# Reordering a scheduled MLP kernel: tile 1 ahead of tiles 2 and 3 at the start, and block 1's layer norm and w2's block sums in other places

## The chip, the cores and the metric

The kernel runs on one core of one Trainium2 chip. The metric is the device time of one execution in microseconds; quoted times are medians of several runs. The span of a profile is shorter than that time by about 1.7 us, because it runs from the first instruction of the program to the last.

## The reference

A layer norm without scale and shift, a matmul to 3584 columns with bias and GELU, and a matmul back to 1024. Inputs are bf16.

```python
B, S, D, F = 1, 2048, 1024, 3584
y = (x - mean(x)) / sqrt(var(x) + 1e-5)
h = gelu_tanh(y @ w1 + b1)
out = h @ w2 + b2
```

## The kernel before

The kernel multiplies blocked matrices with a Strassen-Winograd scheme: seven products instead of eight, paid for with sums of blocks on VectorE. The 2048 rows are two blocks of 1024. A block has eight tiles of 128 rows; `x3`, `stats3`, `norm3` in the text below are the load, the statistics and the normalisation of tile 3. Weights of the first matmul come in chunks.

Instructions are not written in their final order. The program is a graph of tasks. A list scheduler with estimated durations gives every engine its order; TensorE's order is fixed by the program. A packing step, a random search with a seed, decides where buffers lie, and so which task must wait for which earlier user of the same bytes. After that the order of each engine's list is fixed.

```python
SEED = 1                                   # of the packing
ACT_LN = (2, 8, 10, 12, 14)                # tiles whose statistics ScalarE takes
HEAD_LN = (5.0, 7.3, 9.3, 13.5)            # deadlines of the norms of tiles 0 to 3
W2_AT = (...)                              # between which groups w2's block sums are put
DUE_Y = DUE_W = 20.0                       # deadlines of block 1's norm and of those sums

def _simulate(self, pe, dma_bw, dma_lat):
    ...                                    # the ready task with the earliest deadline goes first
    begin = max(now + 0.2, dma_free)       # a load begins when the queue is free

def norm(i):
    if i in ACT_LN:
        ...  # ScalarE: one pass "mean" (1.06 us), one pass "var" (1.15 us), both with accumulator
        ...  # eps on VectorE or GpSimd, rstd (pow) on GpSimd, normalise on VectorE
        return
    ...      # VectorE: two BN_STATS (0.65 us each), BN_AGGR, eps; rstd on GpSimd; normalise

# the head
load_x(0, split=True)
for i in range(1, 8): load_x(i)
for ch in range((RH + 1) // 2): w1_load(0, ch, "A1")
for i in range(4): norm(i)
for bank in range(7): warm(1, bank=bank, full=True)   # 7 matmuls of 512 columns
warm(20)                                               # 20 of 128 columns
for n, c in ((8, c_st[0][0]), (8, c_mv[0]), (6, c_rstd[0])):
    warm(n, c)                                         # 22 more, each set behind a step of tile 0's norm
to_yT_pe(0, 0, (7, 6, 5, 4))                           # tile 0's transposes
...
for t in range(4):
    wave(t, range(0, 3))        # products of tile t with weight chunks 0, 0, 1
    if t < 3: to_yT_pe(0, t + 1, (7,))                 # the next tile's transposes
    wave(t, ...)                # products with the further chunks
...  # then 512-column products, block 0, block 1, and the second matmul
```

The 49 `warm` matmuls do no work; they keep TensorE busy until tile 0 is ready.

## Time and profile before

| | before |
|---|---|
| median of 3 runs | 334.92 us (334.45 to 335.06) |
| span of the profile | 333.3 us |
| TensorE busy | 99% |
| first transposes start | 7.80 us |
| first 512-column product starts | 16.99 us |
| last matmul ends | 330.7 us |

The lines that carry it stand in the prediction. In the chain of waits, each line gives start, length and what was going on; read forward in time it tells at each moment what the end of the kernel was waiting for. `PE` is TensorE, `PEld` its weight loads, `DVE` VectorE, `ACT` ScalarE, `SPq` the queue that issues loads.

### The profile page before, as it was taken

What the parts mean: (1) busy time and instruction counts of PE and PEld (TensorE: products, weight loads), DVE (VectorE), ACT (ScalarE), POOL (GpSimd) and SP (SyncE); (2) the same over time, 40 slices, a digit from 0 to 9 for tenths busy, and PEclk for the clock granted to TensorE, in tenths of its full rate; (3) what the DMA queues carried; (4) which work ended last, traced back from release to release, by engine and by line L of the source; (5) the groups of instructions that cost most, each with busy time, mean ns of one, the idle gap of its engine ahead of it and who ended that gap; (6) DMA issues with size and microseconds to landing.
All of it is one profiled execution on the core that took longest, in us unless ns stands there. A gap on an engine that the chain in (4) does not pass through costs nothing.

```text
span 333.3 us, 6020 instructions
## 1 busy us (share of the span) xinstructions
PE 328.6 (99%) x2328; PEld 220.0 (66%) x2328; DVE 296.6 (89%) x483; ACT 180.3 (54%) x307; POOL 13.8 (4%) x28
## 2 busy tenths in 40 slices
PE   7999999999999999999999999999999999999996
PEld 5944444444444444444446888888888888888885
DVE  4979999999999969985989994799999999999945
ACT  4597999997677676767776554534011222221020
POOL 1310132120000000000000000000000000000000
DMA  8996999999999999999949362644856637569642
GB/s 233 323 219 175 278 276 333 319 244 269 327 278 325 319 327 281 347 350 327 291 133 294 125 201 76 197 139 142 231 160 180 183 110 220 157 176 275 184 121 79
DMA packets 103623, 76.88 MB, mean 231 GB/s; under 512 B 16427, under 2 KB 94891, under 8 KB 103595
## 3 DMA queue, kind: packets, MB, share of 16 engines
q1 hardware_dynamic: 103034, 76.18, 78.3%
q8 instruction: 18, 0.29, 0.4%
q10 hardware_dynamic: 560, 0.33, 0.3%
q14 instruction: 11, 0.08, 0.1%
HBM read 48.96 MB, written 24.38 MB: 220 GB/s over the span
## 4 chain that ended last, share of the span: by engine, by line
PE 96%; DMA 1%; DVE 1%; SPq 0%; POOL 0%; issue 0%
PE ps L903 49%; PE ps L1170 45%; PE ps L1233 2%; DMA mem<-in_x_dram 1%; PE ps L700 0%; DVE st_sb L664 0%; DVE mem L673 0%; POOL rstd_sb L670 0%; SPq L639 0%; DVE mem L1090 0%; SPq L636 0%; PE ps L1192 0%; DVE vpe_sb L667 0%; DVE mv_sb L666 0%; PE ps L1245 0%
## 5 line engine op out<-in xcount | busy, mean ns | idle before, releaser
L903 PE MATMUL ps<-mem 128*128 128x512 f16 x756 | 164.3, 379 | 0.1
L1170 PE MATMUL ps<-mem 128*128 128x256 f16 (+1 forms) x1372 | 150.4, 273 | 0.0
L1170 PEld LDWEIGHTS ps<-mem 128*128 128x128 f16 x1372 | 134.2, 98 | 16.4
L903 PEld LDWEIGHTS ps<-mem 128*128 128x128 f16 (+1 forms) x756 | 73.4, 98 | 89.2 <-ACT mem L833 1.4
L833 ACT COPY mem<-ps 128x512 f32<-128x512 f32 x111 | 64.6, 588 | 75.8 <-PE ps L1170 60.0
L817 ACT ACTIVATE mem<-ps,b_sb 128x512 f16<-128x512 f32 x112 | 74.2, 692 | 23.1 <-DVE ps L841 13.2
L841 DVE TENSOR_TENSOR ps<-ps,mem 128x512 f32<-128x512 f32 x84 | 58.2, 693 | 16.4 <-ACT mem L833 13.0
L1060 DVE TENSOR_TENSOR mem<-mem 128x1792 f16<-128x1792 f16 x56 | 59.8, 1082 | 3.7 <-PE ps L1170 3.5
L778 DVE TENSOR_TENSOR mem<-mem 128x1024 f16<-128x1024 bf16 (+1 forms) x56 | 37.7, 683 | 1.8 <-DMA mem<-in_w_dram 1.7
L969 DVE TENSOR_TENSOR mem<-mem 128x512 f16<-128x512 f16 (+5 forms) x84 | 37.4, 461 | 1.4 <-DMA mem<-in_w_dram 1.1
L1071 DVE TENSOR_TENSOR mem<-mem 128x1792 f16<-128x1792 f16 x32 | 33.6, 1081 | 0.0
L824 ACT COPY ps<-ps 128x512 f32<-128x512 f32 x31 | 17.7, 571 | 26.9 <-PE ps L1170 24.7
L664 DVE BATCH_NORM_STATS2 st_sb<-mem 128x6 f32<-128x512 bf16 x22 | 14.3, 682 | 4.4 <-DMA mem<-in_x_dram 4.4
L1090 DVE TENSOR_TENSOR mem<-ps,mem 128x512 bf16<-128x512 f32 (+1 forms) x25 | 16.2, 663 | 2.2 <-PE ps L1170 1.8
L953 DVE TENSOR_TENSOR mem<-mem 128x2048 f16<-128x2048 bf16 (+1 forms) x16 | 17.3, 1083 | 0.1
L1103 DVE TENSOR_TENSOR mem<-ps,mem 128x512 f32<-128x512 f32 x24 | 16.1, 681 | 0.2
L744 DVE TENSOR_TENSOR mem<-mem 128x512 f16<-128x512 f16 x32 | 12.2, 419 | 1.6 <-DMA mem<-mem 1.4
L670 POOL TENSOR_TENSOR rstd_sb<-vpe_sb,nhalf 128x1 f32<-128x1 f32 x11 | 7.6, 692 | 43.2 <-DVE vpe_sb L667 43.2
L1192 PE MATMUL ps<-ones 128*128 128x128 bf16 (+1 forms) x55 | 6.8, 289 | 1.1 <-POOL ones L605 1.1
L1233 PE MATMUL ps<-mem 128*128 128x128 f16 x112 | 7.3, 219 | 0.0
L1154 ACT COPY ps<-b2d_sb 128x512 f32<-128x512 f32 x6 | 3.5, 590 | 6.0 <-DVE mem L1103 5.8
L869 ACT COPY ps<-mem 128x512 f32<-128x512 f32 x11 | 6.5, 590 | 0.3
(33 smaller groups left out, 64.0 us busy)
## 6 DMA issues: line engine op xcount, KB each, us to landing
mem<-in_w_dram SPq DMA_DIRECT2D x80, 256.0 KB, 5.0
mem<-w_scr SPq DMA_DIRECT2D x28, 448.0 KB, 3.4
w_scr<-mem SPq DMA_DIRECT2D x21, 512.0 KB, 5.4
w_raw<-mem SPq DMA_DIRECT2D x12, 512.0 KB, 5.9
mem<-w_raw SPq DMA_DIRECT2D x12, 448.0 KB, 4.3
mem<-in_w_dram SPq DMA_DIRECT2D x9, 448.0 KB, 4.3
mem<-in_x_dram SPq DMA_DIRECT2D x15, 256.0 KB, 4.4
out_dram<-mem SPq DMA_DIRECT2D x30, 128.0 KB, 3.4
```

What stands on the lines that cost most here:

```text
L778: op("DVE", d_tt(n), lambda e: e.tensor_tensor(out=o[0], in0=a[0], in1=bb[0], op=f), r=[a[1], bb[1]], w=[o[1]], name=f"w1S{k}_{ch}")
L817: op("ACT", A_GELU, lambda e: e.activation(out=dst, in_=bank2(bank), func=ACT.Gelu_apprx_tanh, bias=b1_sb[:, f:f + 1], scale=1.0), r=[bank ...
L824: op("ACT", A_CP, lambda e: e.copy(out=banks[dst][:, :], in_=banks[src][:, :]), r=[bank_c[src]], w=[bank_c[dst]], name=name, lat=A_LAT)
L833: op("ACT", A_CP, lambda e: e.copy(out=v16(a, 0, 2048, F32), in_=banks[src][:, :]), r=[bank_c[src]], w=[a.c()], name=name, lat=A_LAT)
L841: op("DVE", D_PS, lambda e: e.tensor_tensor(out=banks[dst][:, :], in0=banks[src][:, :], in1=v16(a, 0, 2048, F32), op=ALU.add), r=[bank_c[s ...
L903: i = e.matmul(banks[bank][:, :], lhsT=lv[:, k, :], rhs=rv[:, k, :], start=(fresh and k == 0), stop=(k == KH - 1), skip_group_check=True)
L953: op("DVE", d_tt(2 * self.n), lambda e: e.tensor_tensor(out=vd, in0=va, in1=vb, op=ALU.subtract), r=self.cells(a) + self.cells(bb), w=self ...
L969: tt = lambda o, a, c: (lambda e: e.tensor_tensor(out=o, in0=a, in1=c, op=ALU.subtract))
L1060: op("DVE", d_tt(UN // 2), lambda e: e.tensor_tensor(out=v16(t), in0=a[0], in1=bb[0], op=f), r=a[1] + bb[1], w=[t.c()], name=f"in{b}_{p}{q}")
L1071: op("DVE", d_tt(UN // 2), lambda e, va=va, vb=vb, vd=vd: e.tensor_tensor(out=vd, in0=va, in1=vb, op=f), r=h_cells(b, a, u, s) + h_cells(b ...
L1090: op("DVE", 0.08 + n / 960, lambda e: e.tensor_tensor(out=v16(o, 0, 2 * n, BF16), in0=a, in1=bb, op=ALU.add), r=[na, nb], w=[o.c()], name= ...
L1170: i = e.matmul(bank2(bank)[:, t, :], lhsT=av3[:, k, t * P:(t + 1) * P], rhs=bv[:, k, :], start=(fresh and t == ts[0] and k == 0), stop=(t ...
```

## The change

The intent: tile 1 is needed right after tile 0, so its load and its norm go ahead of those of tiles 2 and 3. Block 1's statistics on ScalarE move to other tiles and w2's block sums to other groups, to even out the load of VectorE and ScalarE. `HOLD_LONG` equals `HOLD`, so that line does nothing. `DMA_START` tells the scheduler that from the fourth load on none begins before 2.8 us.

```diff
 HOLD = 0.3
+HOLD_LONG = 0.3
+DMA_START = 2.8
...
-                        begin = max(now + 0.2, dma_free)
+                        n_dma += 1
+                        begin = max(now + 0.2, dma_free, DMA_START if n_dma > 3 else 0.0)
...
-ACT_LN = (2, 8, 10, 12, 14)
+ACT_LN = (2,8,10,13,15)
-W2_AT = ((0, 2, ("A", 2), ("A", 48)), (2, 4, ("A", 48), ("B", 26)), (4, 6, ("B", 26), ("B", 60)), (6, 7, ("B", 60), ("B", 80)))
+W2_AT = ((0,2,("A",0),("A",44)),(2,4,("A",44),("B",26)),(4,6,("B",26),("B",64)),(6,7,("B",64),("B",78)))
-DUE_Y = 20.0
-DUE_W = 20.0
+DUE_Y = 26.0
+DUE_W = 26.0
-SEED = 1
+SEED = 12
-HEAD_LN = (5.0, 7.3, 9.3, 13.5)
-TE_DUE = 7.1
+HEAD_LN = (4.0, 6.2, 11.1, 10.3)
+TE_DUE = 5.0
```

What comes out of it: the same instructions on every engine, TensorE in the same order, the other engines in another order.

More of the change, by code (lines that the diff above doesn't have):

```diff
@@ L359, in _simulate @@
         order = {e: [] for e in ENG}
-        dma_free = 0.0
+        dma_free, n_dma = 0.0, 0
         pe_next = 0
@@ L388, in _simulate @@
                         t = heaps[e][0][2]
-                        if HOLD and any(r < now + HOLD and w.alap < min(t.alap - 0.05, now + 4.0) and r < now + t.dur for r, _, w in waiting[e]):
+                        hold = HOLD_LONG if t.dur > 1.0 and e == "ACT" else HOLD
+                        if hold and any(r < now + hold and w.alap < min(t.alap - 0.05, now + 4.0) and r < now + t.dur
+                                        for r, _, w in waiting[e]):
                             break
@@ L505 @@
 A1_LA, A2_LA, SUM_LA = (12, 12), (12, 12), (6, 7)
-ACT_LN = (2, 8, 10, 12, 14)
+ACT_LN = (2,8,10,13,15)
 UNIT_LA, IN_LA = (6, 5), 5
-W2_AT = ((0, 2, ("A", 2), ("A", 48)), (2, 4, ("A", 48), ("B", 26)), (4, 6, ("B", 26), ("B", 60)), (6, 7, ("B", 60), ("B", 80)))
+W2_AT = ((0,2,("A",0),("A",44)),(2,4,("A",44),("B",26)),(4,6,("B",26),("B",64)),(6,7,("B",64),("B",78)))
 S1_AT = -2
 W2_K = 2
-DUE_Y = 20.0
-DUE_W = 20.0
+DUE_Y = 26.0
+DUE_W = 26.0
 NACC = 5
-Y1_AT, Y1_STEP = -6, 6
+Y1_AT, Y1_STEP = -6,6
 T_PE = 6.0
-SEED = 1
+SEED = 12
 HEAD_DUE = (4.0, 2.0)
-HEAD_LN = (5.0, 7.3, 9.3, 13.5)
-TE_DUE = 7.1
+HEAD_LN = (4.0, 6.2, 11.1, 10.3)
+TE_DUE = 5.0
 OPA = {1: "A11", 2: "A12", 3: "S4", 4: "A22", 5: "S1", 6: "S2", 7: "S3"}
```

## The prediction

> **What bounds the kernel now.** I read the page's busy shares first, then the chain of waits (work that ended last, in order of time), then TensorE's groups after the head, then the timeline of the head, then who waited for whom.
>
> From the page, busy shares by engine:
>
> ```profile
> PE 328.6 (99%) x2328; PEld 220.0 (66%) x2328; DVE 296.6 (89%) x483; ACT 180.3 (54%) x307; POOL 13.8 (4%) x28
> ```
>
> TensorE is busy for 99% of the span, so little can be won without removing matmuls. A busy TensorE may still be a waiting one, so I go to the chain (start us, length us, what):
>
> ```profile
> 1.74 4.38 DMA mem<-in_x_dram
> 6.12 0.02 issue
> 6.15 1.29 DVE st_sb L664 x2
> 7.43 0.64 DVE mem L673 x2
> 8.07 0.13 DVE mv_sb L666
> ...
> 8.22 0.17 DVE vpe_sb L667
> ...
> 8.46 0.56 POOL rstd_sb L670
> 9.05 0.55 DVE mem L673
> ...
> 9.67 0.60 PE ps L700 x8
> ...
> 17.15 12.95 PE ps L903 x60
> 30.10 0.21 PE ps L1192
> 30.32 33.67 PE ps L903 x156
> 63.99 0.03 issue
> 64.01 9.67 PE ps L903 x44
> 73.69 0.03 issue
> 73.71 104.64 PE ps L903 x484
> ...
> 187.05 143.68 PE ps L1170 x1316
> ```
>
> Three things are to be seen. Until 9.67 us the chain is not TensorE but a load of x, then VectorE's layer norm. From 9.67 to 330.73 us it is TensorE, and almost only that. And it breaks twice, at 63.99 and 73.69.
>
> How tight is the TensorE part? 33.67 us / 156 = 215.8 ns per 512-column matmul, 104.64 / 484 = 216.2 ns; 143.68 / 1316 = 109.2 ns per 256-column one. Multiplying out what stands after 17.15 us: 756 x 0.2158 + 1372 x 0.1092 = 163.1 + 149.8 = 312.9 us, against 330.73 - 17.15 = 313.6 us measured. At most some 0.7 us of stalls lie between the head and the end. The two breaks account for part: 9.67 us for 44 matmuls is 44 x 0.2158 + 0.18 us, and the starts of single matmuls in the trace show 0.19 us too much at 63.61 to 64.01 and again at 73.31 to 73.71, 0.39 us together.
>
> So there are three places for a gain: the head up to 17.15 us, those 0.39 us, and the tail after 330.73 us (2.6 us: a last add and a store).
>
> Head, timeline of VectorE and TensorE (start us, length us, engine, line, operation):
>
> ```profile
> 5.16 0.15 DVE L667 TENSOR_SCALAR vpe_sb<-mv_sb 128x1 f32<-128x1 f32 x1
> 5.40 0.56 POOL L670 TENSOR_TENSOR rstd_sb<-vpe_sb,nhalf 128x1 f32<-128x1 f32 x1 [3.86 <-DVE vpe_sb L667]
> 6.15 1.29 DVE L664 BATCH_NORM_STATS2 st_sb<-mem 128x6 f32<-128x512 bf16 x2 [0.83 <-DMA mem<-in_x_dram]
> 7.35 0.72 DVE L673 TENSOR_SCALAR mem<-mem,mv_sb,rstd_sb 128x512 f16<-128x512 bf16 x2
> 7.80 0.72 PE L700 MATMUL ps<-ident,mem 128*128 128x128 f16 x8 [0.80 <-DVE mem L673]
> ```
>
> Tile 0's rstd is ready at 5.96 us, but its normalisation starts at 7.35, because the statistics of tile 1 stand before it in VectorE's order and tile 1 has not landed: VectorE sits idle 0.83 us, until 6.15. That idle time passes to TensorE: tile 0's transposes start only at 7.80. Tile 2, queued before tile 1, landed at about 4.25 us (ScalarE starts on it at 4.27), too early to matter.
>
> **What the Trainium skill says.** "TensorE: Matmul & The Clock Gate", section "Wait — 56ns, not 53.3ns?", gives warm back-to-back starts of N / 2.4 GHz + about 2.5 ns: 55.6 ns for 128 columns, 215.7 ns for 512. The trace agrees: 215.8 here, and 55 to 56 ns between matmuls of the head. The stretch after 17.15 us is therefore at its rate; no new order of other engines can make it faster. "DMA: Bandwidth & Descriptors", section "Queues, rings and completion order", says that descriptors on one DMA engine are consumed in ring order. This case agrees in the head: the queued loads land in the order of issue (4.25, 6.12, 6.87, 7.77 us), so swapping two equal loads should swap their landing times and leave all later ones alone. "DVE: scalar operands, raw-bit mode, write accounting and state across instructions", section "Flops that outlive an instruction", calls VectorE's queue one in-order queue; the normalisation that waits behind the statistics above shows it.
>
> **The change part by part.** I compared the order of instructions of both builds. Each engine executes the same instructions, none added, none removed; TensorE's order is the same throughout. Only the order on VectorE, ScalarE, GpSimd and the load queue changes, and where buffers lie (a new seed of the packing). So nothing is saved in work; only waits can change.
>
> (a) Tile 1's load stands second instead of third. It then lands at about 4.25 us and tile 2 at 6.12; the weights after them stay at 7.77, 8.67, 9.58 and 10.40. Working: statistics of tile 1 follow the row at 5.16 after 0.07 us (the step seen behind other rows of that line), so 5.23 instead of 6.15: 0.92 us earlier. Tile 0's normalisation: 7.35 - 0.92 = 6.43 (rstd at 5.96 is no limit). Transposes of tile 0: 6.88 instead of 7.80. Tile 1's chain (aggregate, rstd, normalise) shifts as well: tile 1's transposes could start at 9.65 - 0.92 = 8.73.
>
> But TensorE needs more than that. The first product of tile 0 with weight chunk 0 would come at 8.64 - 0.92 = 7.72; that chunk lands at 7.77, so 7.82. The third one, which is the first on chunk 1, landed at 8.67, so 8.72 and done at 8.95. TensorE is in order, so tile 1's transposes start at 8.95, not at 8.73: 0.70 us gained instead of 0.92.
>
> (b) Tile 2's statistics on ScalarE now start at 6.14, and its second pass is put behind the two copies of tile 0's transposes: about 7.93 to 9.2. VectorE takes tile 3's statistics (8.59 to 9.88) ahead of tile 2's eps; eps at 9.8, GpSimd's rstd until 10.57, normalised at about 10.6 to 11.15. TensorE gets to tile 2's transposes at about 11.15, so they start at 11.2 instead of 11.85: 0.65 us gained. Tile 3's are not critical. At 17.15 us the kernel is thus some 0.65 us ahead.
>
> (c) What caps it: the first product of the next phase (the one behind the warm-up matmul, 30.15 us) needs VectorE's sums of the transposed tiles 4 to 7. That row starts at 24.25 because the DMA transpose lands then, runs 5.95 us for 16 sums, and the fourteenth, which is needed, ends at 29.53 us: 0.62 us of slack now. The loads and DMA transposes keep their order there, and the queue is full (landings every 0.9 us up to 23.33), so their landing doesn't move with TensorE. The change also puts one more 0.69 us weight sum ahead of them, but it fits the 0.90 us that VectorE sits idle there. So the product can't start before about 29.6: 0.55 us gained of the 0.65.
>
> (d) Block 1's norm: tiles 13 and 15 go to ScalarE instead of 12 and 14; number and cost are equal (1.06 + 1.14 us per tile). Before, these passes stand on ScalarE at 59.04 and 61.16 and at 68.01 and 71.83, in its densest stretch. The PSUM copy that holds up TensorE at 64.01 is the second instruction behind such a pass, the GELU at 73.71 is the one right behind. In the new order tile 13's second pass comes after that GELU, and tile 15's two passes follow at about 76.3 and 77.9, where ScalarE now waits 0.16, 0.18 and 1.16 us for TensorE. I expect both stalls to vanish: 0.39 us, of which I count 0.3, since the passes could bring a small new one.
>
> (e) w2's block sums (1.08 us each on VectorE) start two positions earlier and lie elsewhere. VectorE is at 89%, but the products at 30.15 us aside, the block-1 matmuls have about 0.3 us or more of slack to it. I expect no gain, and a loss of 0 to 0.3 us, counted 0.05.
>
> Sum: 0.55 + 0.3 - 0.05 = 0.8 us. The tail is the same. 334.92 - 0.8 = 334.1 us.
>
> **The rivals.** First, the head gains nothing: VectorE was only one link, and weight chunks 0 and 1 (7.77, 8.67) or tile 2's later chain hold TensorE back. For it: tile 2 is now on ScalarE after 6.14 and its path of two passes and rstd has almost no room. Against: even with these, tile 1's transposes are not later than 8.95. It would leave 334.5 to 334.9. Second, the head gains fully but is given back at 30 us or later to the sums on VectorE, whose start is set by DMA; the slack of 0.62 us says that most stays. If the landings slipped by 0.5 us, the gain would be 0.1 to 0.3 us: 334.6. Third, the new order on VectorE and the new packing make a new wait in blocks 0 and 1 (a block sum ahead of a PSUM add, a load that waits for another buffer's last reader). Every such wait is a direct loss, as TensorE has no slack: 335 to 336. Against it: matmul operands that come by DMA lie ready over 1 us before use everywhere after the head. Fourth, the tail reorders its last stores: the order of the last instructions is the same, so nothing.
>
> **Range and chances.** The repeats of before lie within 0.6 us. Best case, the full 0.65 and both stalls, gives 333.9, with the spread 333.4; the rivals reach 334.9. I take 333.4 to 334.9. A change of 2% would be 6.7 us: on the fast side the whole head up to tile 1's transposes would have to disappear; on the slow side more new stalls would be needed than the kernel has in all. Faster 1%, same 98%, slower 1%.
>
> **What would show it.** In the changed profile: VectorE's statistics of tile 1 at about 5.2 with no wait for x; tile 0's transposes near 6.9, tile 1's near 8.95, tile 2's near 11.2; the phase of 512-column products at 16.3 to 16.6 instead of 16.99; a small wait of TensorE on VectorE's sums near 29.6; no break of the chain near 64 and 74. I am wrong if tile 1 doesn't land near 4.3, if the chain shows a new VectorE or ScalarE link between 30 and 180 us, or if the span falls by less than 0.3 or more than 1.4 us.

## The result, and the profile after

| | before | after |
|---|---|---|
| median, first comparison (6 runs each) | 334.99 us | 334.24 us |
| lowest to highest | 334.44 to 335.33 | 333.73 to 335.32 |
| span of the profile | 333.3 us | 332.0 us |
| first transposes start | 7.80 us | 6.80 us |
| first 512-column product starts | 16.99 us | 16.09 us |
| last matmul ends | 330.7 us | 329.4 us |

The ratio is 0.9982 with a 95% interval of 0.9963 to 1.0. A ratio is the mean time of one kernel's fast runs over that of the other's of the same rounds, so it isn't quite the ratio of the medians. Two later comparisons of the unaltered changed kernel, below, gave 0.9971 (0.9954 to 0.9989) and 0.9985 (0.9969 to 1.0002). The mean of the three, 0.9979, is some 0.7 us.

Line numbers of the changed kernel are 5 higher than those of before; in the kernels of the experiments inserted lines shift them again (L903 of before is L925 where a `HEAD` is put in). Its busy shares:

```profile
PE 328.2 (99%) x2328; PEld 220.2 (66%) x2328; DVE 297.8 (90%) x483; ACT 180.3 (54%) x307; POOL 12.7 (4%) x28
```

The counts of all engines are those of before. The chain of waits of the changed kernel:

```profile
3.15 5.17 DMA mem<-in_w_dram
...
8.37 0.40 PE ps L1238 x4
8.77 0.45 PE ps L705 x8
...
16.26 12.95 PE ps L908 x60
29.21 0.21 PE ps L1197
29.42 147.63 PE ps L908 x684
...
```

Two differences are to be seen. At the start the chain goes over a load of weights (chunk 1, landed at 8.32) instead of a load of x and VectorE's norm. And the piece that began at 30.32 and broke at 63.99 and at 73.69 is now one piece of 147.63 us: 147.63 / 684 = 215.8 ns per matmul, the undisturbed rate.

The head in the timeline of the changed kernel:

```profile
5.00 1.28 DVE L669 BATCH_NORM_STATS2 st_sb<-mem 128x6 f32<-128x512 bf16 x2
6.19 0.72 DVE L678 TENSOR_SCALAR mem<-mem,mv_sb,rstd_sb 128x512 f16<-128x512 bf16 x2
6.80 0.61 PE L705 MATMUL ps<-ident,mem 128*128 128x128 f16 x8
8.37 0.23 PEld L1238 LDWEIGHTS ps<-mem 128*128 128x128 bf16 x4 [0.31 <-DMA mem<-in_w_dram]
8.60 0.61 PE L705 MATMUL ps<-ident,mem 128*128 128x128 f16 x8
```

Tile 1's statistics start at 5.00 without any wait for x, tile 0's transposes at 6.80, and the third product waits for chunk 1, which puts tile 1's transposes at 8.60. That is the mechanism of the prediction. But this profile is of the fastest of its six runs, and the runs of both kernels spread over 1 to 2 us. So I asked which of it repeats, and whether the later part has the cause that I gave it.

### The profile page after: what moved, and what is told of

Its sections match the earlier page's. It is cut to its first block, busy times and chain, and to the rows that moved or that the text cites. A ratio compares the mean times of both kernels' runs of the same rounds, so it can differ in the third digit from the quotient of the medians.

```text
span 332.0 us, 6015 instructions
## 1 busy us (share of the span) xinstructions
PE 328.2 (99%) x2328; PEld 220.2 (66%) x2328; DVE 297.8 (90%) x483; ACT 180.3 (54%) x307; POOL 12.7 (4%) x28
## 4 chain that ended last, share of the span: by engine, by line
PE 97%; DMA 2%; SPq 1%; DVE 0%; issue 0%
PE ps L908 49%; PE ps L1175 45%; PE ps L1238 2%; DMA mem<-in_w_dram 2%; PE ps L705 0%; SPq L644 0%; SPq L772 0%; DVE mem L1095 0%; SPq L641 0%; PE ps L1197 0%; PE ps L1250 0%
## 5 line engine op out<-in xcount | busy, mean ns | idle before, releaser
L1175 PEld LDWEIGHTS ps<-mem 128*128 128x128 f16 x1372 | 134.2, 98 | 16.4
L1095 DVE TENSOR_TENSOR mem<-ps,mem 128x512 bf16<-128x512 f32 (+1 forms) x25 | 16.4, 666 | 2.2 <-PE ps L1175 2.0
L1108 DVE TENSOR_TENSOR mem<-ps,mem 128x512 f32<-128x512 f32 x24 | 16.1, 684 | 0.0
L675 POOL TENSOR_TENSOR rstd_sb<-vpe_sb,nhalf 128x1 f32<-128x1 f32 x11 | 6.6, 598 | 48.0 <-DVE vpe_sb L672 48.0
L678 DVE TENSOR_SCALAR mem<-mem,mv_sb,rstd_sb 128x1024 f16<-128x1024 bf16 (+1 forms) x12 | 6.1, 519 | 0.9 <-POOL rstd_sb L675 0.7
L651 ACT ACTIVATE mem<-mem 128x1024 f16<-128x1024 bf16 x5 | 5.3, 1069 | 2.8 <-DMA mem<-in_x_dram 2.8
```

The costliest lines, as they stand in the source:

```text
L1095: op("DVE", 0.08 + n / 960, lambda e: e.tensor_tensor(out=v16(o, 0, 2 * n, BF16), in0=a, in1=bb, op=ALU.add), r=[na, nb], w=[o.c()], name= ...
L1175: i = e.matmul(bank2(bank)[:, t, :], lhsT=av3[:, k, t * P:(t + 1) * P], rhs=bv[:, k, :], start=(fresh and t == ts[0] and k == 0), stop=(t ...
```

## The experiments

Eight altered kernels, one of them twice, and three repeats of before and after were measured in three batches, each on another chip; each batch had its own runs of before (medians 335.18, 335.50 and 335.37 us, 11 runs each). Below, a stall is the time by which a matmul on TensorE starts later, counted from the start of the one ahead of it, than at the undisturbed rate; I list those of 0.12 us or more between 30 and 175 us. The profile of each kernel is that of one of its runs, so a single stall can be chance; where a kernel was profiled again, or its order shows it, I say so.

**Head alone.** To cut the change cleanly, the start times of the first tasks (up to tile 4's statistics) are overwritten before the orders are fixed, so that all later orders and all buffers stay as they were.

```diff
 # before
+HEAD = {...}      # order of the head's tasks, taken from the changed kernel
 def resolve(self):
+    for h, rows in HEAD.items():
+        for n, s in rows: byname[n].pop(0).start = s
```

> The kernel before with only the order of the first instructions taken from the changed kernel (tile 1's load second, tile 3's statistics ahead of tile 2's eps, tile 2's second ScalarE pass behind tile 0's copies); everything after that, buffers too, as before. My theory (the head and the two ScalarE stalls add up independently): the first 512-column product starts at 16.0 to 16.4 us instead of 16.99, the two breaks of the chain near 63 and 73 us stay at 0.19 us each, and the time falls by 0.6 to 0.9 us against before. Rival (the head's gain is given back at the sums over the transposed tiles 4 to 7, whose start is set by DMA): the head is ahead as above, but the product behind the warm-up matmul still starts near 29.6 to 30.1 and the time falls by 0.1 to 0.4 us.

Measured: 335.03 us, ratio 0.9989 (0.9972 to 1.0006), so a gain is not clear of the noise. The profile is of the slowest of its six runs (335.71). The first 512-column product came at 16.56, the one behind the warm-up matmul at 29.72. Four stalls: 0.21 us at 63.2, 0.28 at 72.9, 0.59 at 77.5 and 0.38 at 83.3. Both old stalls stayed, as expected; the head gained 0.43 us in this profile, less than expected. The time fits the rival's number but not its mechanism: the sum that the rival names ended at 28.90, 0.8 us before the product that needs it. Two things made this profiled run slow: x landed late (statistics of tile 0's second half at 4.44, in before's profile 4.21), and there are two stalls that before's first profile lacks. The one at 83.3 is not the head's: before's second profile has it too (0.38 us at 82.9). Whether the one at 77.5 comes from the head or from chance is open, and so is why the six runs together gained less than expected.

**All but the head.**

```diff
 # after
+HEAD = {...}      # the head's order taken from the kernel before
```

> The changed kernel with the head's order put back to that of before. My theory: the first 512-column product starts at 16.7 to 17.1 us as before, the chain has no break between 30 and 180 us, and the time falls by 0.3 to 0.5 us against before. Rival (the stalls at 64 and 74 us came from the head's timing or from chance, not from where tiles 12 and 14 stand on ScalarE): a break of 0.1 us or more shows again, and the time is that of before within 0.2 us.

Measured: 334.64 us, ratio 0.9981 (0.9962 to 0.9999): 0.54 us under before; my theory had 0.3 to 0.5. The first 512-column product at 17.02. But my theory had no break either, and the profile has two stalls, 0.63 us at 61.1 and 0.16 at 83.3. It is the slowest of six runs (335.52; the others 334.07 to 334.94), and VectorE waited 1.6 us in it for one load of weights. So the two stalls of before near 63 and 73 are gone with the new order (other matmuls than at 61.1), but the new order isn't free of stalls in every run.

**Only the two loads swapped.**

```diff
 # before
 def resolve(self):
+    t1.start, t2.start = t2.start, t1.start     # tasks x1 and x2
```

> The kernel before with nothing but the two loads of tiles 1 and 2 swapped in the queue; all engines keep their order. My theory (the swap needs the other two reorderings): tile 0's transposes start near 6.8 as in the changed kernel, but ScalarE's two passes over tile 2 now start at 5.3 to 6.1 and end at 7.7 to 8.5, ahead of tile 0's copies, so that tile 1's transposes come at 9.2 to 9.9, no earlier than before or hardly; gain 0 to 0.3 us. Rival (the load alone is the lever): tile 1's transposes at 8.6 to 8.9, gain 0.6 us or more.

Measured: 335.07 us, ratio 0.999 (0.9969 to 1.0011). Tile 1's transposes at 9.78, the gain in the expected range. Lines of its timeline:

```profile
7.51 1.15 ACT L651 ACTIVATE mem<-mem,mv_sb 128x1024 f16<-128x1024 bf16 x1
8.66 0.63 ACT L714 COPY mem<-ps 128x256 f16<-128x256 f16 x2
9.11 0.38 PE L1235 MATMUL ps<-mem 128*128 128x128 f16 x4 [0.38 <-DVE mem L711]
```

Tile 2 now lands at 6.31, its second pass keeps ScalarE until 8.66, and only then does ScalarE copy tile 0's transposes; the first product waits until 9.11. The profile puts this wait down to VectorE (L711), whose copies had ended at 8.78; it is ScalarE's first copy that ends just before 9.11. A load that comes earlier is worth little if the engine behind it keeps its old order. One thing was not as expected: tile 0's transposes started at 7.85, not near 6.8, though the first half of tile 0 was normalised by 6.95. The next runs showed why: 29 of the warm-up matmuls ahead of them ran at half rate here.

**The changed kernel again, twice.**

> The changed kernel again, unaltered, for the spread. Expected 0.5 to 1.0 us under before; head at 16.1 to 16.4. If the landing times of the first loads (3.3 to 5.2 us in the first profile, where before had 3.6 to 6.1) belong to the change they come again within 0.1 us; if they are chance they move by 0.2 us or more. The same for the landing of the DMA transposes of tiles 4 to 7 (23.1 to 26.6 us, before 24.2 to 27.5).

> The changed kernel unaltered a third time, beside the next one on the same chip. Expected 0.6 to 1.0 us under before; no stall of TensorE over 0.12 us between 30 and 170 us; tile 1's transposes 0.25 to 0.35 us behind the landing of weight chunk 1, or, if that lands early, set by tile 1's normalisation.

Measured: 334.30 us, ratio 0.9971, and 334.82 us, ratio 0.9985 (0.55 us under before, a little less than expected). No stall of 0.12 us or more between 30 and 175 us in either (the first waits 0.43 us for a load at 179.6). But the head starts the 512-column products at 16.63 and 16.89, not at 16.1 to 16.4. For two different reasons. In the first repeat weight chunk 1 landed at 9.03, not at 8.32. Its timeline on TensorE:

```profile
8.28 0.61 PE L1238 MATMUL ps<-mem 128*128 128x128 f16 x8 [0.51 <-DMA mem<-in_w_dram]
9.07 0.40 PE L1238 MATMUL ps<-mem 128*128 128x128 f16 x4 [0.19 <-DMA mem<-in_w_dram]
9.30 0.61 PE L705 MATMUL ps<-ident,mem 128*128 128x128 f16 x8
```

So landing times of the same kernel move by 0.7 us from run to run; what the first profile had was chance. In the second repeat chunk 1 landed at 7.93, and still tile 1's transposes came at 9.32. Here the engines' busy time from 5 to 7 us tells it (columns: stretch, its length, then for each engine the busy time and in brackets the number of instructions; then granted clock, DMA share, GB/s). Before:

```profile
5.00:7.00 2.00, 2.00 (x35) 1.83 (x33) 1.13 (x4) 1.66 (x4) 0.56 (x1) 1.00 1.08 342
```

The changed kernel, first profile, then its second repeat:

```profile
5.00:7.00 2.00, 2.00 (x39) 2.00 (x38) 2.00 (x6) 1.15 (x2) 0.56 (x1) 1.00 1.05 324
```

```profile
5.00:7.00 2.00, 2.00 (x21) 2.00 (x20) 1.93 (x7) 1.03 (x2) 0.56 (x1) 1.00 1.07 335
```

The same two microseconds hold 35, 39 and 21 matmuls. In the second repeat TensorE was still at half rate: the starts of 28 of the 128-column warm-up matmuls are 107 ns apart, and only from 7.0 us on 56 ns. The 49 warm-up matmuls stand ahead of tile 0's transposes, so they ended at 7.8 us, and the whole microsecond gained by the earlier tile 1 was gone: its chain began

```profile
1.07 6.92 PE ps L1197 x49
8.00 0.24 PE ps L705 x4
```

The granted clock reads 1.00 in all three lines, but that is no measurement: in the two traces of the changed kernel the clock's first record is the begin of full rate (4.91 us in the first profile, 7.07 in the second repeat), before's first profile holds no record of the clock at all, and a stretch without a record is shown as 1.00. The Trainium skill, "TensorE: Matmul & The Clock Gate", section "Part 1: The HAM clock gate (the "warmup" mystery)", says that the clock is at half rate until a busy window of some 3.4 us has passed, that the window is free-running, and that the point moves from run to run. In the eleven traces that record it, full rate begins between 3.90 and 7.11 us, and in 14 profiles between 0 and 29 of the 128-column warm-up matmuls ran at half rate, in four of them 22 or more (one of them of before, whose start at 7.79 it hardly delayed, since tile 0 wasn't ready much sooner).

**The kernel before again.**

> The kernel before, unaltered, for a second profile. Expected: first 512-column product at 16.9 to 17.1 us; stalls of TensorE near 63 and 73 us of 0.15 to 0.3 us each, as in its first profile and in the two kernels that keep its later order; perhaps a third near 83 us of up to 0.4 us, which the first profile lacks and both of those show. If the stalls near 63 and 73 are absent, they are chance and not that order's.

Measured: 335.23 us, ratio 1.0002 (0.9987 to 1.0018). First 512-column product at 16.89; stalls of 0.19 us at 63.5, 0.22 at 73.2 and 0.38 at 82.9. As expected, so the stalls at 63 and 73 belong to the later order of before: four profiles of four have them (both of before, head alone, swap alone). The third shows in three of the four; there the weight load ahead of the matmul waited for a weight sum on VectorE (L778). TensorE's busy time over the stretch that has them, first the kernel before (second profile), then the changed one (second repeat):

```profile
60.00:90.00 30.00, 29.71 (x137) 12.84 (x135) 29.16 (x64) 25.51 (x47) 3.46 (x6) 1.00 1.10 297
```

```profile
60.00:90.00 30.00, 30.00 (x141) 13.45 (x139) 29.79 (x62) 26.81 (x47) 3.81 (x6) 1.00 1.08 291
```

Four matmuls fewer in before, 4 x 0.216 = 0.86 us; VectorE and ScalarE are busy for longer in the changed kernel.

**Only the tiles of ScalarE's statistics.**

```diff
 # before
-ACT_LN = (2, 8, 10, 12, 14)
+ACT_LN = (2, 8, 10, 13, 15)
```

> The kernel before with nothing changed but the tiles of block 1 whose statistics ScalarE takes (13 and 15 instead of 12 and 14); the scheduler then reorders VectorE and ScalarE from about 57 us on; the head stays as before. My theory (those stalls come from the passes over tiles 12 and 14 standing ahead of evacuations in ScalarE's order): no stalls near 63 and 73 us, gain 0.2 to 0.5 us. Rival (the w2 sums' places or the packing removed them): stalls of 0.15 us or more at those places remain, gain under 0.2 us.

Measured: 335.67 us, ratio 1.0013 (0.9997 to 1.0028). The stalls at 63 and 73.2 are gone; in their place are 0.37 us at 69.8 and 0.79 at 72.8, at other matmuls. A further one of 0.36 us at 34.9 is chance as far as the record shows: up to 54 us the instructions of all engines stand in the order of before, which has no stall there. TensorE's weight loads waited, between 32 and 92 us, first in before's second profile, then in this kernel (0.7 us of its 3.1 at 34.9):

```profile
PEld ps L903 <- ACT mem L833: 0.8, 2, 0.5
PEld ps L903 <- ACT mem L817: 0.5, 1, 0.5
```

```profile
PEld ps L903 <- ACT mem L833: 3.1, 5, 1.1
```

My theory falls: moving the tiles alone moves the stalls and, in this profile, makes them larger (1.16 us against 0.40). The rival isn't shown by this either, so the next kernel.

**Only w2's sums, with both deadlines** ("sums alone" below).

```diff
 # before
-W2_AT = (... as before ...)
+W2_AT = (... as changed ...)
-DUE_Y = DUE_W = 20.0
+DUE_Y = DUE_W = 26.0
```

> The kernel before with nothing changed but the places and deadlines of w2's block sums; tiles 12 and 14 stay on ScalarE, the head stays as before. My theory: stalls near 63 and 73 us remain in part (0.1 us or more together), gain 0 to 0.3 us. Rival: they are gone, gain 0.4 us or more.

Measured: 338.22 us (336.90 to 340.59), ratio 1.0096 (1.0061 to 1.013). Both theories wrong: the stalls at 63 and 73 are gone, though tiles 12 and 14 are still on ScalarE, and the kernel lost. The profile has 0.28 us at 68.5, 0.41 at 80.0, and then one stall of 2.26 us at 83.0, at the same matmul that waits up to 0.38 us there in before. What TensorE waited for, and its stretches behind the stall:

```profile
PE ps L903 <- DVE mem L778: 2.1, 1, 2.1
```

```profile
86.00:90.00 4.00, 4.00 (x12) 1.46 (x11) 3.89 (x10) 0.69 (x2) 0.65 (x1) 0.57 0.99 312
90.00:93.00 3.00, 3.00 (x15) 1.37 (x14) 2.82 (x7) 2.83 (x5) 0.00 (x0) 1.00 1.25 290
```

A weight sum on VectorE (L778) came late. It waited 0.98 us for a load that landed at 84.7; the load had been issued at 78.5, where before issues its own at 74.0, because it stood in the queue behind a DMA transpose of tile 12, whose normalisation came later on VectorE (70.1 us, in before 64.5). `DUE_Y` is the deadline of block 1's normalisations, so that delay may be the deadline's work and not the sums'; the two were not separated. And here the stall cost twice: from 86.3 to 89.7 us the granted clock is one half, matmul starts are 427 ns apart instead of 216, another 1.7 us. This isn't so in every run: the clock fell in two of the four (339.00 and 340.59 us, mean clock 0.995); the other two, at full rate throughout, took 337.44 and 336.90, still more than before.

**The tiles put back, and the packing put back, in the changed kernel.**

```diff
 # after, first kernel
-ACT_LN = (2,8,10,13,15)
+ACT_LN = (2, 8, 10, 12, 14)
 # after, second kernel
-SEED = 12
+SEED = 1
```

> The changed kernel with only the tiles of ScalarE's statistics put back to 12 and 14. Theory A (the new tiles and the new places of the w2 sums are needed together, as each alone gave no gain: +0.2 to +0.4 and +3 us against before): stalls of TensorE come back between 60 and 90 us, 0.3 to 3 us in sum, and the time is at or above that of before. Theory B (the new head or the new packing keeps the w2 sums' new places from doing harm): stalls under 0.3 us in sum, time within 0.4 us of the changed kernel's.

> The changed kernel with only the packing's seed put back, so that buffers lie elsewhere and the scheduler orders around other reuse waits from about 40 us on. Theory A (the packing is part of what makes it free of stalls): stalls of 0.3 us or more between 35 and 90 us, time 0.3 us or more above the changed kernel's. Theory B (packing indifferent): within 0.3 us of the changed kernel's.

Measured: 336.71 us, ratio 1.0037 (1.002 to 1.0054), and 336.87 us, ratio 1.0044 (1.0021 to 1.0067). In the first four stalls, 0.47, 0.42, 0.35 and 0.84 us, 2.1 us in all. In the second one stall of 2.36 us at 94.0, just behind the stretch that I had named, and again half a clock after it (of its four runs only in the profiled one, 337.93 us; the others took 335.92 to 337.24). VectorE and TensorE in the second:

```profile
95.80 0.69 DVE L783 TENSOR_TENSOR mem<-mem 128x1024 f16<-128x1024 bf16 x1 [2.11 <-DMA mem<-in_w_dram]
```

```profile
96.50:100.00 3.50, 3.46 (x9) 1.23 (x10) 3.47 (x7) 0.69 (x1) 0.00 (x0) 0.51 1.10 380
```

VectorE's instructions around this sum are the same and in the same order in the changed kernel, where the sum starts at 92.28 with no wait; what differs is its load, which comes later (landed at 95.77 instead of 92.02; the first of its group was issued at 88.07 instead of 86.08). Theory A holds for both in time, if not in the place of the second's stall. Of the combinations tried, only those with the new tiles, the new places and the new packing together have profiles free of stalls (the changed kernel's three and the two of the next version; not that of all but the head). That does not show that they need one another: the seed belongs to a random search, no third seed was run, and a schedule that was picked for being good may lose by any alteration.

**A version with weight chunks 0 and 1 ahead of tile 3, twice.** Since chunk 1's landing held the head, the loads go in the order tiles 0, 1, 2, chunk 0, chunk 1, tile 3; on VectorE tile 2's eps and normalisation go back among tile 3's statistics.

```diff
 # after
+HEAD = {...}    # SP: x0 x1 x2 w_chunk0 w_chunk1 x3 ...; DVE: norm1 eps2 stats3_0 norm2 stats3_1 ...
```

> The changed kernel, with weight chunks 0 and 1 loaded ahead of tile 3 (order: tiles 0, 1, 2, chunk 0, chunk 1, tile 3), and tile 2's eps and normalisation put back among tile 3's statistics on VectorE so that they don't wait for the later tile 3. My theory (in the changed kernel the head is held by the landing of chunk 1: tile 1's transposes start 0.28 us after it in both its profiles, 8.32 to 8.60 and 9.03 to 9.30): chunk 1 lands at 7.3 to 8.2, tile 1's transposes start at 8.45 to 8.75 whenever it does, set by tile 1's normalisation, tile 2's at 10.8 to 11.1, and the time is 0.1 to 0.5 us under the changed kernel's. Rival (tile 2's path over ScalarE holds the head): tile 2's transposes stay at 10.95 to 11.5 and the time doesn't change.

> The version with weight chunks 0 and 1 ahead of tile 3 once more, for a direct comparison with the changed kernel. If the head gains what its first profile shows (first 512-column product at 16.14, the changed kernel's at 16.09 and 16.63), it is 0.1 to 0.4 us faster than the changed kernel; if the gain is swallowed by the spread of the later stages, 0 within 0.2 us.

Measured: 334.19 us, ratio 0.9974 (0.9961 to 0.9987), and 334.33 us, ratio 0.9966 (0.9953 to 0.9979). The second was in the same rounds as the changed kernel's 334.82 and 0.9985: 0.5 us less in the medians, 0.0019 x 335 = 0.6 us less in the means, but the intervals overlap (0.9979 above 0.9969). Both intervals are against before; taken directly, the six runs and the other six differ by 0.58 us with a standard error of 0.21. So it is likely, from this one comparison, that it is faster than the changed kernel. Chunk 1 landed at 7.31 and 8.02. The first profile's timeline on TensorE:

```profile
7.83 0.83 PE L1255 MATMUL ps<-mem 128*128 128x128 f16 x12
8.81 0.62 PE L722 MATMUL ps<-ident,mem 128*128 128x128 f16 x8
```

No product waits for a load any more, and tile 1's transposes follow 0.06 us behind its normalisation (8.75), a little later than the 8.45 to 8.75 expected. In the second, 22 of the 128-column warm-up matmuls ran at half rate and tile 0's transposes began at 7.51; tile 1's at 8.99. There the cap of my prediction showed for the first time: the sum that the product at 29.83 needs ended at 29.77, a stall of 0.14 us. But it was not the DMA transposes that held the sums; the first had landed at 23.35. VectorE came to them late, behind its own weight sums (L800):

```profile
21.84 2.74 DVE L800 TENSOR_TENSOR mem<-mem 128x1024 f16<-128x1024 bf16 x4
24.49 5.95 DVE L766 TENSOR_TENSOR mem<-mem 128x512 f16<-128x512 f16 x16
```

The obvious next step, fewer warm-up matmuls ahead of tile 0's transposes, was not run; whether full rate would then come later is open.

## Why the prediction was right, and where its steps were not

The time: 334.1 predicted, 334.24, 334.30 and 334.82 measured, all within the range of 333.4 to 334.9. Of the steps behind the number, the head's is right in its path; (c), (d) and (e) are not, and that their errors nearly cancelled is luck.

- **What bounds the kernel.** Right. Undisturbed, TensorE takes 215.8 ns per 512-column matmul in both kernels, and all the gain came from the head and from stalls.
- **(a) Tile 1's chain, with chunk 1 as the next limit.** Right where the clock was at full rate in time: 8.32 to 8.60 and 9.03 to 9.30, a distance of 0.28 us as predicted (8.67 to 8.95). Wrong in saying that the other landings stay: chunk 1 landed at 8.32, 9.03 and 7.93 in three profiles of one kernel. And a limit was missing: the warm-up matmuls in front of the transposes, which take the gain when full rate comes late.
- **(b) Tile 2 at 11.2.** 10.95, 11.50 and 11.74 measured, 2.20 to 2.42 us behind tile 1's transposes where I had 2.25: right, and it moves with tile 1.
- **(c) The cap at the sums over tiles 4 to 7.** Wrong for the changed kernel: those sums ended at 28.78, 29.08 and 29.19 and not at 29.53, 0.5 to 0.9 us before use, so nothing was capped. Nor is their start set by the DMA transposes alone, as I had it: in the changed kernel's first profile the first had landed at 23.10, and VectorE began the row at 23.50, behind its own weight sums. The transposes of before's first profile had landed late by chance (24.22 for the first; 23.1 to 23.9 in the changed kernel, 23.8 in before's second profile). The size was still near: over the six profiles with the new engine order in the head (three of the changed kernel, head alone, tiles back, packing back) the product behind the warm-up matmul starts at 29.64 us in the mean, over the five with the old one (two of before, all but the head, tiles alone, sums alone) at 30.05. The ranges overlap (29.26 to 30.05 and 29.88 to 30.19). So the head is worth about 0.41 us where I had 0.55. The sums didn't take the rest; late landings and the late clock, seen in single profiles above, are the likely cause.
- **(d) The two stalls vanish because tiles 13 and 15 take the place of 12 and 14.** The stalls vanished in all three profiles, but not for the reason given: they are gone as well in the two kernels that keep tiles 12 and 14 on ScalarE with the new places of the sums (sums alone, tiles back), and the new tiles alone gave 1.16 us of stalls at other matmuls. One reading was off too: the copy that held up TensorE at 64.01 is the third instruction behind the pass (copy, GELU, copy), not the second.
- **(e) w2's sums: 0.05 us.** The step that failed most clearly. Without the other parts, but with both deadlines, they cost 2.7 us; without them (tiles alone) nothing is gained (1.0013, 0.9997 to 1.0028). The slack of 0.3 us that I had named isn't there: with before's later order, three of four profiles have a matmul at 83 us that waits 0.36 to 0.38 us for a weight sum, and this wait grew to 2.26. The cost of a sum was misread as well: 1.08 us is that of other sums (L1060, L1071); those of w2's blocks take 1.22, 0.68 and 0.42 us (L953, L969).
- **The sum.** From the product behind the warm-up matmul to the end of the last matmul, before's later order took 300.56, 300.98, 301.68 and 300.89 us, the new one 300.16, 300.58, 300.23 and 301.02 (all but the head): 0.53 us in the mean, where I had 0.3 - 0.05; with four values each and a range of 0.9 to 1.1 us that is an estimate. With the head 0.94 us; the times say 0.7. The total was right, but I had added parts as if each had its own worth. (d) and (e) had none alone in the kernels run.
- **The rivals.** The third (new waits by the new order or packing, 335 to 336 us and more) did not come in the changed kernel, but new stalls came in each of the four kernels that take only part of the later change, three of them clearly slower than before. What spoke against it in the prediction, that matmul operands lie ready over 1 us before use, was beside the point: in the two kernels with a stall of over 2 us the load that mattered was one that VectorE's sum waits for.

What stays open: why the landings of the first loads vary by over 1 us between runs (in the three profiles of the changed kernel tile 1 lands at 4.18 to 4.24, the next load, tile 2, at 4.86 to 6.30, and the loads behind it follow that one); what the seed of the packing changes for the better; and which of the new places and the two deadlines does what. The seed alone in before, other seeds, and the changed kernel with w2's sums or one deadline put back were not run.

## What to carry to other kernels

In a kernel whose bounding engine has no slack, judge a new order of the other engines as a whole: here parts of a good order, taken alone, were no better than the old one or worse. Before moving work forward at the start, look at what stands in front of it on the bounding engine, warm-up matmuls included, and at the landing time of the next operand; and read more than one profile, since a landing or a clock that differs by 1 us makes the wrong step look like the limit. A long stall can cost more than its length: here two of over 2 us on TensorE were each followed by 3.4 us at half rate, though not in every run of the same kernel.

## What the Trainium skill lacked or had wrong

- "TensorE: Matmul & The Clock Gate", the table of the clock's states, gives an idle window of about 3.4 us for the fall to half rate. Here stalls of 2.26 and 2.36 us were enough (sums alone, packing back): starts 427 ns apart for 3.41 us, 1.7 us lost each time. Stalls of up to 0.84 us did not do it. In these two traces full rate began at 4.38 and 4.41 us and fell to half at 86.30 and 96.57, which is 24.0 and 27.0 times 3.41 us later; counted in such steps, each stall lay wholly in the last one before the fall and left TensorE idle for about two thirds of it. That this share decides is my inference from two cases.
- The same page says of the start that for modelling the ramp is under 1% of a typical span, and not to be fitted to a count of slow matmuls. That holds (1 us of 335), but here that 1 us was the whole gain in the head: with 28 half-rate warm-up matmuls tile 0's transposes began at 7.83 us instead of 6.80.
- No page that I found says that a trace may hold no record of the clock before the first full-rate moment, or none at all: the stretch from 5 to 7 us read 1.00 with 21 matmuls in it and with 39. At the start, count matmuls or look at the distance of their starts.
- "DMA: Bandwidth & Descriptors" says that descriptors are consumed in ring order, and the head's loads on SyncE's queue did land in order in all profiles. It doesn't say how far such a landing moves between runs of one kernel: the sixth load of that queue (weight chunk 1) landed between 7.93 and 9.03 us in three profiles.
